# Attention and routed feed-forward on one core: slots in partitions, centred keys, token tiles of 128, ranks from sign counts

## The chip, the cores and the metric

The kernel runs on one core of one Trainium2 chip. A core has five engines that take their instructions in order and wait for each other through semaphores: PE (TensorE, matmul), DVE (VectorE), ACT (ScalarE), POOL (GpSimd) and SP, which here only issues transfers. The metric is device time in microseconds (us) of one execution.

## What is computed

Eight batches, eight heads, 576 tokens, head dimension 64, 32 memory slots. Keys and values are summed into slots, every token attends over the 32 slots, the heads are joined to rows of 512, and the 128 best rows of each batch go through a two-layer feed-forward network.

```python
a = np.exp(phi - np.max(phi, axis=2, keepdims=True))
a = a / (np.sum(a, axis=2, keepdims=True) + 1e-09)
k_m = np.einsum('bhsm,bhsd->bhmd', a, k)
v_m = np.einsum('bhsm,bhsd->bhmd', a, v)
scores = scale * np.matmul(q, k_m.transpose(0, 1, 3, 2))
scores = scores - np.max(scores, axis=-1, keepdims=True)
attn = np.exp(scores)
attn = attn / (np.sum(attn, axis=-1, keepdims=True) + 1e-09)
x = np.matmul(attn, v_m)              # then heads joined: (B, S, 512)
gate = np.einsum('bsd,d->bs', x, w_gate)
top_idx = np.argpartition(-gate[b], capacity)[:capacity]      # per batch, capacity 128
xe = x[b, top_idx]
ye = np.maximum(xe @ w1, 0.0) @ w2    # w1 512x1024, w2 1024x512
out[b, top_idx] = xe + sigmoid(gate[b, top_idx])[:, None] * ye
```

## The kernel before

The program has three stages. In the first, 16 groups (a batch and four heads) go through a long softmax of phi on DVE (`softmax`) and a sum of keys into slots (`keys`, L298), two groups at a time; `values(0)` sums the values of batches 0 to 3 beside the second half of them. In the second stage `values(1)` does the same for batches 4 to 7 while batches 0 to 3 go through attention and feed-forward. In the third, batches 4 to 7 go through attention and feed-forward with nothing beside them.

`values` is 144 steps of 16 matmuls (L336, four row strips of 32 rows each); its operands come in 18 chunks of 8 steps from `vparts` and `aparts` in DRAM, through the queues of SP and POOL (L317, L323), two chunks in buffers.

A batch is a generator that runs from `yield` to `yield` (37 of them): `centre` (the mean of v_m over slots is taken apart as a high and a low row), then three times `scores` and `attend` (two columns of 96 tokens each), `rank`, `gather`, `ffn1`, `ffn2`. In `scores` tokens lie in partitions: 16 matmul instructions (L405; every fp32 matmul in the code is two instructions on PE), a maximum, a subtraction, Exp and Tanh (exp(s)-1 is built as (exp(s)+1)·tanh(s/2)), a product, a sum and a reciprocal. In `attend` the result is transposed on PE (L445), copied by ACT (L447), multiplied with the centred values (L453), scaled by DVE (L456), the two mean rows are added by POOL (L460), and DVE takes the product with w_gate and its sum (L430, L432, L435). `rank` counts for each token the tokens above it (L487) and the equal ones before it (L489); `gather` turns ranks into indices (L500, L505) and fetches the 128 rows; `ffn1` takes their gate again, transposes them (L530) and multiplies with w1 (L539, hidden units in partitions), `ffn2` with w2 (L552).

The order on every engine is the order in which the generators are advanced: `turns(jobs, 10, 3)` gives each of up to three live batches one step per round and starts a new one at the earliest 10 rounds after the last; in the second stage `beside(..., sums, 1)` puts one step of `values` behind every step of a batch. All matmul results but those of `values` share four PSUM banks (`bank`). "Column" below is a group of tokens; "step" is what lies between two yields.

## Time and profile before

| | us |
|---|---|
| time, median of 3 runs (1300.88 to 1302.33) | 1301.61 |
| the profiled execution's own time | 1302.55 |
| its span in the trace | 1300.8 |
| first stage, up to the last key sum | 652 |
| second stage, up to the end of batch 3 | 652 to 1016.3 |
| third stage, batches 4 to 7 | 1016.3 to 1296.4 |

The span is the time from the program's first instruction to its last; the profiled execution's own time is 1.75 us longer. The stage ends are the ends of instructions in the trace: the last matmul of L298, and the feed-forward result (L556) of batch 3 and of batch 7. The granted clock of PE is given as a share of 2.4 GHz, so that 0.50 is its lower level, 1.2 GHz, and 1.00 its upper; the trace's first record of a change is at 840 us, and the column says 1.00 for all that lies ahead of that.

### The profile page before, as it was taken

The page shows a single profiled execution, that of the slowest core. Times are in us where ns is not written, and L with a number is a line of the kernel's source. Part 1 is how long each engine was busy: PE and PEld are TensorE (multiplying, and loading weights), DVE is VectorE, ACT ScalarE, POOL GpSimd, SP SyncE. Part 2 cuts the span into 40 slices and gives each one's busy share as a digit, 9 for nine tenths or more (in the row PEclk, how much of TensorE's full clock was granted, in tenths as well). Part 3 has the DMA queues.
Part 4 walks back from the last instruction along what each step waited for, and adds up shares of the span by engine and source line. Part 5 has one row for each costly group of instructions (what it writes and reads, how often), then busy time and mean ns, then how long its engine had stood idle before and what let it go on. Part 6 is the DMA issues. An engine that isn't in the chain of part 4 may idle for free. (4 is left out here: it accounts for less than half of the span.)

```text
span 1300.8 us, 16837 instructions
## 1 busy us (share of the span) xinstructions
PE 691.2 (53%) x6656; PEld 589.1 (45%) x6656; DVE 875.1 (67%) x1480; ACT 272.0 (21%) x489; POOL 406.5 (31%) x489
## 2 busy tenths in 40 slices
PE   0021022221248877773209989879986653557646
PEld 0011011111148767663108778758766443436524
DVE  8978799999789999999703465543524467664551
ACT  1222133333133333333102111101100221012100
POOL 7133332111244324421232343533440034321230
PEclk9999999999999999999999999975895766677677
DMA  5799871211379996962185565553660121100010
GB/s 191 287 319 365 305 265 46 58 34 54 94 157 193 185 195 145 199 143 53 37 247 133 139 135 130 122 132 87 145 179 21 33 61 41 40 21 21 29 33 17
DMA packets 119934, 165.48 MB, mean 127 GB/s; under 512 B 84912, under 2 KB 86960, under 8 KB 115248
## 3 DMA queue, kind: packets, MB, share of 16 engines
q1 hardware_dynamic: 93360, 84.69, 26.9%
q0 software_dynamic: 26496, 79.72, 20.5%
q8 instruction: 53, 0.87, 0.3%
q14 instruction: 25, 0.20, 0.1%
HBM read 105.64 MB, written 68.16 MB: 134 GB/s over the span
## 5 line engine op out<-in xcount | busy, mean ns | idle before, releaser
L336 PE MATMUL acc<-v_rows,a_rows 32*128 32x128 f32 x4608 | 255.4, 396 | 92.4 <-DMA a_rows<-aparts 92.4
L336 PEld LDWEIGHTS acc<-v_rows,a_rows 32*128 32x128 f32 x4608 | 237.6, 305 | 123.2 <-issue 109.3
L276 PE MATMUL bank<-ident,e 128*96 128x128 f32 x96 | 23.9, 422 | 345.8 <-DVE e L245 345.8
L276 PEld LDWEIGHTS bank<-ident,e 128*96 128x96 f32 x96 | 16.8, 193 | 348.7 <-issue 300.0
L460 POOL TENSOR_TENSOR xj<-xj,mean 96x1024 f32<-96x1024 f32 x48 | 118.1, 2465 | 126.5 <-DVE xj L456 108.9
L323 POOL DMA_DIRECT2D a_rows<-aparts x144 | 90.1, 633 | 214.2 <-PE acc L336 202.6
L288 POOL DMA_DIRECT2D aparts<-alo x64 | 47.7, 746 | 238.4 <-DVE alo L284 212.2
L298 PE MATMUL bank<-aS,kb 96*128 96x64 f32 x384 | 86.1, 423 | 11.6 <-ACT aS L278 11.6
L298 PEld LDWEIGHTS bank<-aS,kb 96*128 96x128 f32 x384 | 83.1, 331 | 16.4 <-ACT aS L278 15.7
L453 PE MATMUL bank<-vbd,eT 128*96 128x256 f32 x192 | 76.4, 551 | 14.0 <-ACT eT L447 14.0
L539 PE MATMUL bank<-xeT,w_sb 128*128 128x128 f32 x512 | 77.6, 325 | 8.5 <-ACT xeT L533 8.5
L539 PEld LDWEIGHTS bank<-xeT,w_sb 128*128 128x128 f32 x512 | 75.5, 239 | 12.0 <-ACT xeT L533 11.7
L430 DVE TENSOR_TENSOR prod<-xj,wg 96x1024 f32<-96x1024 f32 x24 | 37.8, 1574 | 47.0 <-POOL xj L460 47.0
L456 DVE TENSOR_TENSOR xj<-bank,rd 96x512 f32<-96x512 f32 x48 | 32.4, 682 | 53.4 <-PE bank L453 53.4
L405 PE MATMUL bank<-kbd,qb 128*96 128x64 f32 x384 | 58.6, 337 | 0.0
L410 DVE TENSOR_REDUCE smx<-bank 96x16 f32<-96x512 f32 x24 | 16.3, 678 | 61.3 <-PE bank L405 61.3
L405 PEld LDWEIGHTS bank<-kbd,qb 128*96 128x96 f32 x384 | 56.4, 249 | 1.9
L552 PE MATMUL bank<-w_sb,hT 128*128 128x512 f32 x128 | 56.6, 595 | 0.0
L556 DVE SCALAR_TENSOR_TENSOR ye<-bank,gr,xe 128x512 f32<-128x512 f32 x8 | 6.0, 750 | 74.2 <-PE bank L552 74.2
L453 PEld LDWEIGHTS bank<-vbd,eT 128*96 128x96 f32 x192 | 40.9, 232 | 31.3 <-ACT eT L447 15.1
L190 DVE SCALAR_TENSOR_TENSOR lo<-num,vh 128x576 f32<-128x576 f32 x48 | 36.2, 755 | 21.7 <-ACT vh L151 21.7
L505 PE MATMUL bank<-tok,pick 96*128 96x1 f32 x96 | 20.4, 340 | 56.9 <-DVE pick L500 56.9
(131 smaller groups left out, 1374.2 us busy)
## 6 DMA issues: line engine op xcount, KB each, us to landing
v_rows<-vparts SPq DMA_DIRECT2D x72, 512.0 KB, 6.1
vparts<-vb POOLq DMA_DIRECT2D x32, 576.0 KB, 5.5
vparts<-vhi POOLq DMA_DIRECT2D x32, 576.0 KB, 7.2
kb<-in_k SPq DMA_DIRECT2D x16, 576.0 KB, 7.7
vb<-in_v SPq DMA_DIRECT2D x16, 576.0 KB, 6.3
aparts<-aparts POOLq DMA_DIRECT2D x32, 288.0 KB, 3.2
a_rows<-aparts SPq DMA_DIRECT2D x144, 64.0 KB, 7.1
a_rows<-aparts POOLq DMA_DIRECT2D x144, 64.0 KB, 6.4
```

Source lines behind the costliest of these rows:

```text
L190: stt(out=lo, in0=val, scalar=GRID, in1=h, op0=ALU.mult, op1=ALU.subtract)
L276: nc.tensor.transpose(out=tp[:, c], in_=a[:, (c0 + c) * PT:(c0 + c + 1) * PT], identity=ident)
L288: nc.gpsimd.dma_start(out=aparts[r, u, b, part, 0].rearrange("(c p) m -> p c m", p=PT), in_=src[:, :, h * M:(h + 1) * M])
L298: nc.tensor.matmul(out=km[:, rr], lhsT=kb[:, c, rr * P:(rr + 1) * P], rhs=aS[:, c, rr * 2 * M:(rr + 1) * 2 * M], start=(c == 0), stop=(c = ...
L323: (nc.sync, nc.gpsimd)[u].dma_start(out=a_rows[ch % 2][2 * r + u::8, :, r].bitcast(F32), in_=aparts[r, u, b0:b0 + SET].rearrange("b t w s ...
L336: nc.tensor.matmul(out=accs[bb][:, :P].rearrange("p (u d) -> p u d", d=Dh), lhsT=ar[p, s].rearrange("p r m -> p (r m)"), rhs=vr[p, :, s], ...
L405: nc.tensor.matmul(out=sc[:, c, :, r], lhsT=qb[:, r, c * PT:(c + 1) * PT], rhs=kbd[b][:, r], start=True, stop=True)
L430: nc.vector.tensor_mul(prod[:n, :cols], rows, wg[:n].unsqueeze(1).to_broadcast([n, cols, D]))
L453: nc.tensor.matmul(out=o[:, u].rearrange("p r d -> p (r d)"), lhsT=eT[:, c, u], rhs=vbd[b % 3][:, u], start=True, stop=True)
L460: nc.gpsimd.tensor_add(x, x, t.unsqueeze(1).to_broadcast([PT, 2, D]))
L539: nc.tensor.matmul(out=ps[:, f, :n], lhsT=w1_sb[:, d, (f0 + f) * P:(f0 + f + 1) * P], rhs=xeT[:, d, :n], start=(d == 0), stop=(d == KD - 1))
L552: nc.tensor.matmul(out=ps[:n], lhsT=hT[:, f, :n], rhs=w2_sb[:, f], start=(f == 0), stop=(f == KF - 1))
```

## The change

The attention part is laid out anew, with slots in partitions.

- `centre` subtracts from k_m its mean over the slots (three DVE operations), so that scores come out centred, and no maximum is taken. The small remainder of the value mean is cut into three bf16 pieces by POOL (`los`), which PE adds to each output with one bf16 matmul (`ones3`, `rest`); the large part is one row, added by POOL.
- `scores` has k_m as the stationary operand and 288 tokens as the moving one: per batch 16 matmul instructions (L452), each with 64 output partitions, ACT reads them from PSUM (four Exp, four Tanh), and DVE's product lands as the transposed tile `eT`. The PE transposes of L445 and ACT's copies of L447 are gone.
- `attend` takes the sums over slots on PE (`den`, 20 instructions with 4 columns) and works on five tiles of 128 tokens, the last one half filled.
- `rank` counts with ACT's Sign, five times, and with DVE's comparison for equal, five times. `gather` brings the gate along with the index, so that the gate of the fetched rows isn't taken again.
- `ffn` multiplies with w1 with tokens in partitions (16 instructions of 512 columns instead of 64 of 128), transposes the result on PE and copies it by ACT. w1 and w2 are cut by a `yield` after every four instructions.
- Batches start 14 rounds apart instead of 10; a batch has 39 yields. The first step of `values(1)` now stands ahead of batch 0's first transpose on PE.
- At the end a count (`good`) says whether any sum over slots was too large; then all engines read it and, if it was, jump into a second path (`general=True`) that takes every batch again with a maximum.

The core of the diff (removed lines are the functions above):

```diff
-    for t in kbd + vbd:
+    vls = [const.tile([P, NPR, 2, M], F32, name=f"vls{i}") for i in range(2)]
+    for t in kbd + vbd + vls:
         nc.gpsimd.memset(t, 0.0)
...
     def late_consts():
...
+        nc.vector.tensor_copy(ident16, ident)
...
+        for t in tgs:
+            nc.gpsimd.memset(t, 0.0)
+            nc.gpsimd.iota(t[:, :, 0], pattern=[[P, NT]], base=0, channel_multiplier=1,
+                           allow_small_or_imprecise_dtypes=True)
...
     def centre(b):
+        heads = kbd[b].rearrange("p r (u m) -> p (r u) m", u=2)
+        km = work.tile([P, H], F32, name="kmean")
+        nc.vector.tensor_reduce(km, heads, axis=AX.X, op=ALU.add)
+        nc.vector.tensor_scalar_mul(km, km, 1.0 / M)
+        nc.vector.tensor_sub(heads, heads, km.unsqueeze(2).to_broadcast([P, H, M]))
+        yield
...
+        los = work.tile([P, NPR, 3], BF16, name="los")
+        for i in range(3):
+            nc.gpsimd.tensor_copy(los[:, :, i], lo)
+            if i < 2:
+                nc.gpsimd.tensor_sub(lo, lo, los[:, :, i])
+        yield
...
+    def expm1(dst, s, shape):
+        e = step.tile(shape, F32, name="es")
+        d = step.tile(shape, F32, name="th")
+        nc.scalar.activation(e, s, AF.Exp, scale=scale)
+        nc.scalar.activation(d, s, AF.Tanh, scale=scale / 2)
+        yield
+        nc.vector.scalar_tensor_tensor(out=dst, in0=e, scalar=1.0, in1=d,
+                                       op0=ALU.add, op1=ALU.mult)
+    def scores(b):
+        N = S // 2
+        for j in range(2):
+            qb = qs.pop((b, j))
+            for g in range(2):
+                sc = bank([P, N])
+                for rr in range(2):
+                    nc.tensor.matmul(out=sc[rr * 2 * M:(rr + 1) * 2 * M], lhsT=kbd[b][:, 2 * g + rr],
+                                     rhs=qb[:, 2 * g + rr], start=True, stop=True)
+                yield from expm1(eTs[b % 2][:, g, j * N:(j + 1) * N], sc, [P, N])
...
+    def attend(b, general):
...
+        den = bank([P, NT, 2, 4])
+        for c in range(NT):
+            for g in range(2):
+                nc.tensor.matmul(out=den[:, c, g], lhsT=eT[:, g, c * P:(c + 1) * P], rhs=heads_of,
+                                 start=True, stop=True)
+        yield
...
+        for c0 in range(0, NT, 2):
+            cols = min(2, NT - c0)
+            x = step.tile([P, 2, D], F32, name="xj", bufs=3)[:, :cols]
+            for c in range(cols):
+                o = bank([P, D])
+                nc.tensor.matmul(out=o, lhsT=ones3, rhs=rest, start=True, stop=False)
+                for g in range(2):
+                    nc.tensor.matmul(out=o[:, g * 4 * Dh:(g + 1) * 4 * Dh],
+                                     lhsT=eT[:, g, (c0 + c) * P:(c0 + c + 1) * P],
+                                     rhs=vbd[b % 3][:, g], start=False, stop=(g == 1))
+                yield
...
+            nc.gpsimd.tensor_add(x, x, row.unsqueeze(1).to_broadcast([P, cols, D]))
+            yield
+            score(tg[:, c0:c0 + cols, 1], x, cols)
...
     def rank(b):
...
+        for c in range(NT):
+            g = tg[:, c, 1:2]
+            off = (NT - 1 - c) * P
+            nc.scalar.activation(sign, row, AF.Sign, bias=g, scale=-1.0,
+                                 accum_out=less[:, c:c + 1])
             nc.vector.scalar_tensor_tensor(
+                out=cmp, in0=row, scalar=g, in1=wide[:, off:off + S],
                 op0=ALU.is_equal, op1=ALU.mult, accum_out=equal[:, c:c + 1])
+            if c % 2:
+                yield
...
+    def ffn(b, t):
...
+        for f0 in range(0, F, 512):
+            ps = bank([P, 512])
+            for d in range(KD):
+                nc.tensor.matmul(out=ps[:n], lhsT=xeT[:, d, :n], rhs=w1_sb[:, d, f0:f0 + 512],
+                                 start=(d == 0), stop=(d == KD - 1))
+                if d % 2:
+                    yield
+            nc.scalar.activation(h[:n, f0:f0 + 512], ps[:n], AF.Relu)
         hT = one.tile([P, KF, P], F32, name="hT")
         for f0 in range(0, KF, 4):
+            turned(hT, h, f0, f0 + 4)
             yield
         ps = bank([P, D])
         for f in range(KF):
             nc.tensor.matmul(out=ps[:n], lhsT=hT[:, f, :n], rhs=w2_sb[:, f],
                              start=(f == 0), stop=(f == KF - 1))
+            if f % 2:
+                yield
...
+    def attention_and_ffn(b, general=False):
+        if not general:
+            for j in range(2):
+                load_q(b, j)
         yield from centre(b)
         yield
+        yield from (scores_less_max if general else scores)(b)
...
-    finish(beside(turns([batch(b) for b in range(SET)], 10, 3), sums, 1))
+    finish(beside(turns([attention_and_ffn(b) for b in range(SET)], 14, 3), sums, 1))
     finish(sums)
-    finish(turns([batch(b) for b in range(SET, B)], 10, 3))
+    finish(turns([attention_and_ffn(b) for b in range(SET, B)], 14, 3))
+    ps = bank([1, B])
+    nc.tensor.matmul(out=ps, lhsT=ones, rhs=good, start=True, stop=True)
...
+    taken = nc.values_load(any_bad[0:1, 0:1])
+    with tc.If(taken > 0):
+        for b in range(B):
+            finish(attention_and_ffn(b, True))
```

On PE in the third stage, before, around the feed-forward of one batch (xe, w_sb and hT are the feed-forward's; gate is another batch's ranks, kbd and es a third batch's scores, pick its ranks' selection):

```order
L475 MATMUL bank<-ident,gate 96x96 x6
L405 MATMUL bank<-kbd_90,qb 96x2x32 x8
L530 MATMUL bank<-ident,xe 128x128 x4
L539 MATMUL bank<-xeT,w_sb 128x128 x32
L445 MATMUL bank<-ident,es 128x96 x4
L552 MATMUL bank<-w_sb,hT 128x512 x8
L453 MATMUL bank<-vbd_92,eT 96x256 x4
L350 MATMUL bank<-ident,v_m_8604 128x128
L445 MATMUL bank<-ident,es 128x96 x4
L505 MATMUL bank<-tok,pick 128x1 x6
```

The same place after the change, w2 of one batch (L622) beside the scores of another (L452), and the rank transposes of a third (L538) with their selection (L575) behind:

```order
L452 MATMUL bank<-qb,kbd_90 64x288 x2
L622 MATMUL bank<-w_sb,hT 128x512 x2
L538 MATMUL bank<-ident,tg_128 128x128 x4
L538 MATMUL bank<-ident,tg_128 128x64
L452 MATMUL bank<-qb,kbd_90 64x288 x2
L622 MATMUL bank<-w_sb,hT 128x512 x2
L452 MATMUL bank<-qb,kbd_90 64x288 x2
L622 MATMUL bank<-w_sb,hT 128x512 x2
L452 MATMUL bank<-qb,kbd_90 64x288 x2
L622 MATMUL bank<-w_sb,hT 128x512 x2
L575 MATMUL bank<-tg_128,pick 128x2 x5
```

Before, w1 and w2 of a batch stand as one piece each; now w2 is in four pieces with the scores of another batch between them, and the transposes of L445 are gone.

On DVE, the end of the last batch's ranks before (cmp above and cmp equal in turn):

```order
L489 SCALAR_TENSOR_TENSOR cmp,equal<-row,gate,wide 96x288
L487 TENSOR_SCALAR cmp,above<-row,gate 96x576
L489 SCALAR_TENSOR_TENSOR cmp,equal<-row,gate,wide 96x384
L487 TENSOR_SCALAR cmp,above<-row,gate 96x576
L489 SCALAR_TENSOR_TENSOR cmp,equal<-row,gate,wide 96x480
L487 TENSOR_SCALAR cmp,above<-row,gate 96x576
L489 SCALAR_TENSOR_TENSOR cmp,equal<-row,gate,wide 96x576
L493 TENSOR_TENSOR above<-above,equal 96x6
L500 TENSOR_TENSOR pick<-iota_r,above 96x768
```

and a batch's ranks on DVE after the change:

```order
L485 TENSOR_REDUCE tg_126<-four 128x1
L556 SCALAR_TENSOR_TENSOR cmp,equal<-row,tg_126,wide 128x576 x5
L562 SCALAR_TENSOR_TENSOR less<-less,equal 128x5
L570 TENSOR_TENSOR pick<-iota_r,less 128x640
L579 TENSOR_SCALAR idx<-bank 128x1
L587 TENSOR_SCALAR gr<-gr 128x1
L627 SCALAR_TENSOR_TENSOR ye<-bank,gr,xe 128x512
```

The counts of the tokens above have left DVE for ACT, and between the index and `ye` the gate of the fetched rows is no longer taken.

On PE at the program's end, after the change (before, it ends with L552 and a branch):

```order
L611 MATMUL bank<-w_sb,xeT 128x512 x8
L600 MATMUL bank<-ident,h 128x128 x8
L622 MATMUL bank<-w_sb,hT 128x512 x8
L708 MATMUL bank<-good,ones 1x8
L714 TENSOR_LOAD any_bad
L715 COMPARE_AND_BRANCH
```

A matmul, a load and a compare stand behind the last feed-forward; the load waits for the last transfers of all queues, and it and the compare stand at the end of every engine.

## Rows read from the trace of the kernel before

**Rows 1.** The page: busy time by engine, and PE's granted clock in 40 slices

```profile
PE 691.2 (53%) x6656; PEld 589.1 (45%) x6656; DVE 875.1 (67%) x1480; ACT 272.0 (21%) x489; POOL 406.5 (31%) x489
...
PEclk9999999999999999999999999975895766677677
```

**Rows 2.** Busy us by stretch: stretch, its length, engines, granted clock, DMA share, GB/s

```profile
0.00:652.00 652.00, 236.23 (x2783) 224.28 (x2783) 569.81 (x848) 188.98 (x307) 206.50 (x323) 1.00 0.60 166
652.00:690.00 38.00, 8.16 (x93) 6.56 (x92) 2.91 (x14) 2.97 (x9) 9.49 (x15) 1.00 0.90 252
690.00:840.00 150.00, 141.66 (x1381) 116.20 (x1378) 77.95 (x152) 20.80 (x43) 62.53 (x58) 1.00 0.57 131
840.00:1016.30 176.30, 148.85 (x1624) 118.15 (x1623) 70.38 (x149) 18.95 (x42) 51.96 (x49) 0.76 0.43 104
1016.30:1296.40 280.10, 156.27 (x784) 123.91 (x783) 154.03 (x317) 40.26 (x88) 75.02 (x44) 0.70 0.11 33
```

**Rows 3.** PE's waits from 1000 us on: total us, times, longest

```profile
PE bank L505 <- DVE pick L500: 45.7, 4, 15.6
PE bank L475 <- DVE gate L435: 35.6, 5, 9.8
PE bank L453 <- ACT eT L447: 14.0, 6, 4.8
```

**Rows 4.** Timeline of PE: start us, us, what, [idle before <-releaser]

```profile
682.61 1.97 PE L336 MATMUL acc<-v_rows,a_rows 32*128 32x128 f32 x32 [29.84 <-DMA a_rows<-aparts]
...
701.30 2.02 PE L453 MATMUL bank<-vbd,eT 128*96 128x256 f32 x4
703.25 1.12 PE L336 MATMUL acc<-v_rows,a_rows 32*128 32x128 f32 x16
704.30 0.47 PE L350 MATMUL bank<-ident,v_m 128*128 128x128 f32 x1
...
711.93 2.82 PE L405 MATMUL bank<-kbd,qb 128*96 128x64 f32 x16
...
720.72 0.90 PE L445 MATMUL bank<-ident,es 96*128 96x96 f32 x4
...
833.80 6.45 PE L539 MATMUL bank<-xeT,w_sb 128*128 128x128 f32 x29 [0.69 <-ACT xeT L533]
...
847.89 7.13 PE L552 MATMUL bank<-w_sb,hT 128*128 128x512 f32 x16
854.96 1.11 PE L336 MATMUL acc<-v_rows,a_rows 32*128 32x128 f32 x32
...
873.08 2.69 PE L505 MATMUL bank<-tok,pick 96*128 96x1 f32 x12 [4.69 <-DVE pick L500]
...
885.07 1.09 PE L389 MATMUL bank<-ident,vsum 128*96 128x128 f32 x4
```

**Rows 5.** Groups by line, shapes apart: busy us, mean ns | idle before

```profile
L460 POOL TENSOR_TENSOR xj<-xj,mean 96x1024 f32<-96x1024 f32 x48 | 118.1, 2465 | 126.5 <-DVE xj L456 108.9 <-issue 15.7
L487 DVE TENSOR_SCALAR_CACHE_REDUCE cmp<-row,gate 96x576 bf16<-96x576 f32 x48 | 37.7, 785 | 4.8 <-ACT row L477 4.3
L417 DVE SCALAR_TENSOR_TENSOR es<-es,d 96x512 f32<-96x512 f32 x24 | 16.4, 684 | 38.9 <-ACT d L415 38.9
L151 ACT ACTIVATE vh<-num,c 128x576 int16<-128x576 f32 x16 | 12.4, 774 | 10.1 <-DVE num L180 10.1
L164 DVE TENSOR_SCALAR ph<-ph,mx 128x576 f32<-128x576 f32 x16 | 22.3, 1397 | 0.6
```

**Rows 6.** Timeline: DVE's start, and the last batch's end

```profile
4.77 14.45 DVE L164 TENSOR_SCALAR ph<-ph,mx 128x576 f32<-128x576 f32 x1
...
1276.62 1.11 PE L530 MATMUL bank<-ident,xe 128*128 128x128 f32 x4 [4.63 <-DMA xe<-out,idx]
1295.62 0.75 DVE L556 SCALAR_TENSOR_TENSOR ye<-bank,gr,xe 128x512 f32<-128x512 f32 x1 [16.86 <-PE bank L552]
1296.65 1.02 POOL L558 DMA_INDIRECT out<-ye,idx  x1 [22.40 <-DVE ye L556]
```

More of the change, by code (lines that the diff above doesn't have):

```diff
@@ L57 @@
     PT = S // NC
-    NJ = qT.shape[1]
-    NPR = qT.shape[3]
+    NPR = qT.shape[2]
+    NT = -(-S // P)
+    tiles = [min(P, S - c * P) for c in range(NT)]
     NG = phiT.shape[1]
@@ new lines, in centre @@
+        yield
+        rest = work.tile([3, D], BF16, name="rest")
+        tp = bank([3, NPR, P], BF16)
+        for r in range(NPR):
+            nc.tensor.transpose(out=tp[:, r], in_=los[:, r], identity=ident16)
+        nc.scalar.activation(rest, tp.rearrange("p r d -> p (r d)"), AF.Copy)
+        mean[b] = row, rest
+    st = {}
+    def expm1(dst, s, shape):
[6 more added lines that the diff above has]
+                                       op0=ALU.add, op1=ALU.mult)
@@ new lines, in rank @@
+    def rank(b):
+        tg = tgs[b % 3]
+        row = one.tile([P, S], F32, name="row")
+        for c0 in range(0, NT, 4):
+            cc = range(c0, min(c0 + 4, NT))
+            ps = bank([P, 4 * P])
+            for c in cc:
+                n = tiles[c]
+                nc.tensor.transpose(out=ps[:, (c - c0) * P:(c - c0) * P + n],
+                                    in_=tg[:n, c, 1:2].to_broadcast([n, P]),
+                                    identity=ident[:n, :n])
+            n = sum(tiles[c] for c in cc)
+            nc.scalar.activation(row[:, c0 * P:c0 * P + n], ps[:, :n], AF.Copy)
+        yield
+        less = work.tile([P, NT], F32, name="less")
+        equal = work.tile([P, NT], F32, name="equal")
+        sign = one.tile([P, S], BF16, name="sign")
+        cmp = one.tile([P, S], BF16, name="cmp")
+        for c in range(NT):
[3 more added lines that the diff above has]
+                                 accum_out=less[:, c:c + 1])
+            nc.vector.scalar_tensor_tensor(
+                out=cmp, in0=row, scalar=g, in1=wide[:, off:off + S],
+                op0=ALU.is_equal, op1=ALU.mult, accum_out=equal[:, c:c + 1])
+            if c % 2:
+                yield
+        yield
+        nc.vector.scalar_tensor_tensor(out=less, in0=less, scalar=-0.5, in1=equal,
+                                       op0=ALU.mult, op1=ALU.add)
+        st[b, "rank"] = less
```

292 lines of the change are left out of this document (121 added, 171 removed).

## The prediction

> **What bounds the kernel now.** I read the page first, then busy time by stretch, then waits and the timeline of PE. The page [rows 1] shows no engine near its limit over the span (DVE 67%, PE 53%), so each stage is read by itself [rows 2]. The first is DVE's: 569.8 of 652 us. The change leaves it alone. In the second, PE first waits 29.8 us for its operands (682.61) [rows 4], and from 690 to 840 it is busy 141.7 of 150 us, from 840 to 1016.3 for 148.9 of 176.3, while DVE has about half the time: PE sets the pace. In the third none does: PE is busy 156.3 of 280.1 us, DVE 154.0, POOL 75.0 [rows 2]. There PE waits 45.7 us for rank selections, 35.6 us for gates and 14.0 us for the copied transposes [rows 3], behind chains of DVE, POOL and ACT. So in the second stage the change is worth what it does to PE, in the third also what it takes from the chains.
>
> PE has two prices, by its clock. The granted clock reads 1.00 up to 840 us only because nothing is recorded there: four L453 take 1.95 us at 701.30 (to the next row's start), and 32 of L336 take 1.11 us at 854.96 where 16 took 1.05 us at 703.25 [rows 4]. Up to about 840 PE ran at the lower level, 1.2 GHz, busy with L336 and short pieces of attention between them; the level rose during the first w1 matmuls, which began at 833.80 [rows 4]. Behind that the granted clock is 0.76 on average to 1016.3 and 0.70 in the third stage [rows 2], which is the upper level for 52% and 40% of the time.
>
> **PE's work.** In lower-level us per batch, from [rows 4], before: scores 48 x 0.172 (2.75/16) = 8.3; L445 12 x 0.21 = 2.5; L453 24 x 0.488 = 11.7; w1 64 x 0.222 = 14.2; w2 16 x 0.88 (twice 7.07/16, measured at the upper level) = 14.1; selection 12 x 0.224 = 2.7; 20 other transposes x 0.26 (L389) = 5.2. Sum 58.7. With 144 steps of 1.05 us, 151, the second stage comes to 386; the trace's busy time there, its upper-level share counted twice, is 141.7 + 148.9 x 1.52 = 368, so the prices are good to 5%.
>
> After: den 20 x 0.224 (L505's price, as few columns) = 4.5; outputs 5 x (1.95 + 0.44 for the bf16 matmul, half an L552) = 12.0; w1, now of w2's shape, 14.1; w2 14.1; selection 10 x 0.224 = 2.2; 28 transposes x 0.26 (5 of ranks, 8 of h new) = 7.3. Scores are 16 instructions of 288 columns: by L453's price per column 0.549 each, 8.8; but two neighbours write different halves of the array's outputs. No row shows that; the nearest is L336, four of which with a quarter of the rows each go in 0.26 us. I take the halves as overlapping, 4.4, since that row is nearest in kind. Sum 58.6, or 63.0 without overlap (35 lower-level us over eight batches, some 22 us of time).
> The Trainium skill, "TensorEngine Tiling (Array Packing)", Key Properties, says that such tiles work in parallel but that a change of tiling mode drains the engine; here every score step changes mode. By its first half the sum is the one taken; no row here prices the drain.
>
> So PE's work stays the same. What changes is its clock and its idle time.
>
> **The other engines.** DVE has 154.0/4 = 38.5 us per batch. It loses three of four passes over scores (each three times about 0.684, L417's shape; 6.2), most of L417 itself (0.5), L487 (6 x 0.86 with its accumulator read, 5.2) and the second gate (about 1.9), gains 2 in centre and den, and sweeps five tiles instead of six: about 26. POOL has 18.8 and loses 3.5 of 6 adds of 2.46 us [rows 5]: about 11 with `los`. ACT has 10 and gains five Signs of about 0.85 (0.774 for 576 columns [rows 5] and an accumulator read): about 14. All stay under PE's 29 (upper) to 59 (lower).
>
> **First stage and start of the second: +6 us.** DVE's first instruction is now the copy of `ident16`. The first L164 took 14.45 us, the other fifteen about 0.52 [rows 5, 6], while POOL filled its buffers. The copy will sit there in its place, with the maximum and L164 behind it: +2 (0 to 5). Then 0.8 MB more of q goes ahead of the first operands on SP: at 252 GB/s [rows 2] 3.2 us, with issue 4. PE starts at 688.6 instead of 682.6. The POOL memsets of `eT` wait for the end of the first stage as the copies ahead of them do: nothing.
>
> **Second stage: 17 us less.** The first w1 comes behind 45 steps of `values` instead of 72, since batches start 14 rounds apart: 45 x 1.05 = 47.3, batch 0's work without feed-forward 28.3, batch 1's first 16 steps 19.0, idle 4; with 5 us of w1 until the clock rises (6 at 833.80) that is 792. Of 386 lower-level us 286 are left, plus 28 idle as before in 840 to 1016.3 (176.3 - 148.9). With the clock shared as before, 52% upper, (286 + 28)/1.52 = 207: batch 3 ends at 999 instead of 1016. A step of `values` stands between every two pieces of w1 (3.5 us each), which can keep the level low; den is one more long row of small matmuls like the selection, during which PE was at the lower level at 873.08 [rows 4]. Against that, PE has fewer gaps. Bounds for the share: 0.25 (+45 us) and 0.75 (-27).
>
> **Third stage: 74 us less.** PE's busy time stays 156 x 58.6/58.7. Idle was 124. It should fall to 50: 12 while batch 4 is alone (centre is a chain of DVE operations that PE waits for), 10 in the next 14 rounds, 5 for each of two rounds with three batches (selection waits behind `ye`), 4 and 14 at the drain, where the last batch's fetch (4.6 us [rows 6]), copies and ReLU stand alone. Gates and ranks now have PE work of two other batches to hide them, and their chains are shorter by L487, half the POOL adds and the second gate. Bounds 30 to 124. 156 + 50 = 206.
>
> **The end: +5 us.** After the last `ye` every engine waits for the last scatter (4.4 us to the span's end now, as before), then loads a register, compares and jumps over the second path. No row shows these; the nearest are a semaphore step of under 0.1 us and a fetched gather of 4.6 us. I take one such round trip, 5, since all of it is serial; bounds 0 and 10.
>
> Sum: 999 + 206 + 4.4 + 5 = 1214 us of span; with 1.75 around it 1216 for a profiled execution, whose like now is 0.9 above the median: **1215**.
>
> **Rivals.**
> 1. *The clock stays low in the second stage.* The steps of `values` between the pieces of w1 keep PE at 1.2 GHz to the end of batch 3, as from 690 to 840, where PE hardly paused. Then 314 us follow 792: 1106, and 1322 in all: slower. It decides at an upper-level share below 7%. For it: w1 ran in pieces of 6 us before and in 3.5 now. Against it: at 833.80 the level rose within one such piece [rows 4], and pieces of 3.5 us with 1 us between are most of PE's time there. 6%.
> 2. *Hand-offs stay.* With four banks and in-order queues PE's idle time in the third stage stays 124: 999 + 280 + 10 = 1289. For it: `ye` still stands ahead of the next selection on DVE. Against it: the chains lose half their work. 9%.
> 3. *PE at the upper level throughout,* now that gaps are few: 386/2 + 32 from 688.6, 913, then 117 + 50, and the end: 1090. Against it: 690 to 840, where it was 94% busy at the lower level. 4%.
> The Trainium skill, "TensorE: Matmul & The Clock Gate", "Why this matters for your kernels", promises the upper level to an engine kept busy without gaps; the stretch from 690 to 840 [rows 2] speaks against it as a rule for small matmuls, and I leave it this rival's 4%.
> 4. *It doesn't do what it says:* the count finds a bad sum and the second path runs, eight batches one after the other, over 2000 us. The sums are 32 and a small rest here. 1%.
>
> **How the numbers follow.** The forecast has 80%. Its own range is 1165 (share 0.75 and 30 idle, about) to 1275 (share 0.25, no overlap of scores' halves in part). To 1290 it takes in rival 2; outside are rivals 1, 3 and 4 and some 7% of the forecast. A measurement tells 0.2% from no change (2.6 us). Faster 92%, slower 7% (rivals 1 and 4), within 1%.
>
> **What would show it.** PE's first operand wait should end near 689; the first w1 at about 787; batch 3's result at 999, batch 7's at 1205; PE idle 50 us in the third stage, with the waits for selection and gates gone from the top; four neighbouring score instructions in 1.1 us at the lower level (2.2 without overlap); DVE near 26 us per batch. Wrong would be: a granted clock of 0.5 through 800 to 1000, PE waiting for DVE as long as now, or a tail of over 15 us behind the last `ye`.

## The result, and the profile after

| | before | after |
|---|---|---|
| time, median of four runs, us | 1301.24 | 1172.95 |
| lowest and highest, us | 1299.97, 1302.33 | 1165.39, 1177.25 |
| ratio to before, 95% interval | | 0.901 (0.896 to 0.906) |
| profiled execution's span, us | 1300.8 | 1175.4 |
| PE's first step of `values(1)`, us | 682.6 | 687.4 |
| end of batch 3, of batch 7, us | 1017.1, 1296.4 | 974.6, 1165.9 |

The change saves 128 us, 9.9%; 87 were forecast. The time lies near the lower end of the forecast's range. The ends of batches here are the ends of the feed-forward's last DVE instruction, 0.75 us behind its start (the 1016.3 us given ahead for batch 3 is its start). The profiled execution, to which all traces of the change belong, is the slowest of its four. The page after, in the lines that answer to [rows 1]:

```profile
PE 662.3 (56%) x6138; PEld 492.3 (42%) x6138; DVE 765.7 (65%) x1283; ACT 293.0 (25%) x561; POOL 351.3 (30%) x529
...
PEclk9999999999999999999999999999577987598897
```

Busy time by stretch, as [rows 2]: first stage, PE's wait for its operands, second stage up to the first recorded rise of the clock, its rest up to batch 3's end, third stage, tail. Columns: stretch, length, busy us of PE, PEld, DVE, ACT and POOL, granted clock, DMA share, GB/s.

```profile
0.00:654.20 654.20, 236.39 (x2784) 224.40 (x2784) 568.80 (x849) 189.09 (x307) 209.44 (x337) 1.00 0.59 165
654.20:687.40 33.20, 0.37 (x2) 0.19 (x2) 1.04 (x3) 0.44 (x2) 9.72 (x17) 1.00 0.90 254
687.40:783.00 95.60, 93.56 (x888) 69.58 (x888) 37.27 (x83) 15.61 (x40) 26.79 (x40) 1.00 0.59 139
783.00:974.65 191.65, 182.80 (x1949) 116.13 (x1945) 60.73 (x131) 37.20 (x89) 57.97 (x79) 0.83 0.57 132
974.65:1165.90 191.25, 149.15 (x525) 81.98 (x525) 97.62 (x217) 50.62 (x123) 46.39 (x56) 0.81 0.16 52
1165.90:1175.40 9.50, 0.00 (x0) 0.00 (x0) 0.23 (x3) 0.00 (x0) 0.99 (x1) 0.65 0.11 37
```

PE's idle time is what is to be seen: 8.8 of 191.7 us in the second stage behind 783 us (before 27.5 of 176.3 from 840 us on), 42.1 of 191.3 in the third (before 123.8 of 280.1), at a higher granted clock (0.83 and 0.81 for 0.76 and 0.70). PE's waits from 1000 us on, as [rows 3]:

```profile
PE bank L575 <- DVE pick L570: 10.9, 4, 5.3
PE bank L411 <- DVE vls L401: 8.5, 3, 6.5
PE bank L600 <- DMA xe<-out,idx: 5.4, 1, 5.4
PE bank L538 <- DVE tg L485: 5.0, 2, 3.4
```

The selection (L575, before L505) went from 45.7 to 10.9 us, the gates (L538, before L475) from 35.6 to 5.0, and the copied transposes (14.0) are gone. The third stage after begins 25 us ahead of this window; with them the only wait that grows is L411's, for the centring of values, to 13.6 us, and it is then the largest. PE's timeline at the start of the second stage, as [rows 4]:

```profile
687.42 1.12 PE L353 MATMUL acc<-v_rows,a_rows 32*128 32x128 f32 x16 [32.85 <-DMA a_rows<-aparts]
...
698.16 1.23 PE L452 MATMUL bank<-qb,kbd 128*64 128x288 f32 x4
699.32 1.12 PE L353 MATMUL acc<-v_rows,a_rows 32*128 32x128 f32 x16
...
707.85 4.43 PE L493 MATMUL bank<-heads_of,eT 128*128 128x4 f32 x20
712.20 1.12 PE L353 MATMUL acc<-v_rows,a_rows 32*128 32x128 f32 x16
713.12 0.65 PE L510 MATMUL bank<-rest,ones 3*128 3x512 bf16 x1
713.70 2.08 PE L512 MATMUL bank<-vbd,eT 128*128 128x256 f32 x4
715.70 1.12 PE L353 MATMUL acc<-v_rows,a_rows 32*128 32x128 f32 x16
```

From start to start four score instructions (L452) take 1.16 us, the 20 of `den` 4.35, and an output tile (L510 and L512) 2.58.

**One sum for each stage.** In what follows "work" is PE's busy time with the part at the upper clock level counted twice, so in lower-level us, and "upper" is the busy time at the upper level; both come from the trace's clock records and the busy time between them. Then length = work - upper + idle. The work of two traces with the same instructions differs by up to 4% (401.9 us in the second stage of e7 below, which has the change's instructions there, and 386.3 in e2's). The forecast's upper is what its other numbers leave: 386 less the busy 278 (310.4 less 32 idle), and 234 less 156.

| | second stage: length | work | upper | idle | third stage: length | work | upper | idle |
|---|---|---|---|---|---|---|---|---|
| before | 334.5 | 382.7 | 84.7 | 36.5 | 279.3 | 226.9 | 70.7 | 123.1 |
| forecast | 310.4 | 386 | 108 | 32 | 206 | 234 | 78 | 50 |
| after | 287.2 | 399.5 | 123.1 | 10.9 | 191.3 | 244.4 | 95.3 | 42.1 |
| e3 chains back | 290.9 | 398.8 | 118.5 | 10.6 | 221.5 | 244.7 | 87.0 | 63.8 |
| e4 before, order of after | 333.3 | 392.6 | 100.5 | 41.1 | 258.9 | 226.9 | 75.5 | 107.6 |
| e6 scores by tokens | 372.1 | 416.2 | 83.8 | 39.7 | 235.5 | 266.4 | 93.1 | 62.1 |
| e9 the same with a yield | 337.5 | 422.6 | 116.3 | 31.2 | 239.0 | 265.2 | 86.2 | 60.0 |
| e10 pauses | 318.7 | 407.6 | 120.8 | 31.9 | 222.1 | 248.4 | 87.6 | 61.3 |

### The profile page after: what moved, and what is told of

It reads as the page before. It is cut to its first block, busy times and chain, and to the rows that moved or that the text cites. A ratio compares the mean times of both kernels' runs of the same rounds, so it can differ in the third digit from the quotient of the medians.

```text
span 1175.4 us, 15823 instructions
## 1 busy us (share of the span) xinstructions
PE 662.3 (56%) x6138; PEld 492.3 (42%) x6138; DVE 765.7 (65%) x1283; ACT 293.0 (25%) x561; POOL 351.3 (30%) x529
## 5 line engine op out<-in xcount | busy, mean ns | idle before, releaser
L611 PE MATMUL bank<-w_sb,xeT 128*128 128x512 f32 x128 | 73.0, 709 | 3.4 <-ACT xeT L602 3.4
L519 POOL TENSOR_TENSOR xj<-xj,mean 128x1024 f32<-128x1024 f32 (+1 forms) x24 | 47.7, 1988 | 73.0 <-DVE xj L516 72.9
L512 PE MATMUL bank<-vbd,eT 128*128 128x256 f32 x160 | 66.4, 556 | 0.0
L516 DVE TENSOR_TENSOR xj<-bank,rd 128x512 f32<-128x512 f32 x40 | 27.6, 689 | 56.8 <-PE bank L512 56.6
L622 PE MATMUL bank<-w_sb,hT 128*128 128x512 f32 x128 | 62.3, 620 | 0.2 <-ACT hT L602 0.2
L480 DVE TENSOR_TENSOR prod<-xj,wg 128x1024 f32<-128x1024 f32 (+1 forms) x24 | 25.1, 1046 | 46.6 <-POOL xj L519 46.6
L211 DVE TENSOR_TENSOR low<-low,lo 128x576 f32<-128x576 f32 x64 | 48.5, 758 | 2.2
L305 POOL DMA_DIRECT2D aparts<-ahi x64 | 47.7, 745 | 2.1 <-DMA a_rows<-aparts 1.6
L209 DVE TENSOR_TENSOR lo<-lo,rh 128x576 f32<-128x576 f32 x64 | 48.0, 750 | 0.0
L512 PEld LDWEIGHTS bank<-vbd,eT 128*128 128x128 f32 x160 | 38.4, 265 | 18.7 <-issue 13.7
L556 DVE SCALAR_TENSOR_TENSOR cmp<-row,tg,wide 128x576 bf16<-128x576 f32 x40 | 32.7, 817 | 17.7 <-ACT row L542 16.8
```

Of the source, the lines that this page charges most:

```text
L209: tt(out=lo, in0=lo, in1=rh, op=ALU.mult)
L211: tt(out=low, in0=low, in1=lo, op=ALU.add)
L305: nc.gpsimd.dma_start(out=aparts[r, u, b, part, 0].rearrange("(c p) m -> p c m", p=PT), in_=src[:, :, h * M:(h + 1) * M])
L512: nc.tensor.matmul(out=o[:, g * 4 * Dh:(g + 1) * 4 * Dh], lhsT=eT[:, g, (c0 + c) * P:(c0 + c + 1) * P], rhs=vbd[b % 3][:, g], start=False, ...
L516: nc.vector.tensor_mul(x[:, c].rearrange("p (h d) -> p h d", d=Dh), o.rearrange("p (h d) -> p h d", d=Dh), rd[:, c0 + c].unsqueeze(2).to_b ...
L519: nc.gpsimd.tensor_add(x, x, row.unsqueeze(1).to_broadcast([P, cols, D]))
```

## The experiments

Each starts from the changed kernel unless its heading says otherwise; times are medians of four runs or five, ratios are to the kernel before, run beside them.

### Order or chains

The prediction gave PE's lost idle time two reasons at once, another batch's work beside each wait and shorter chains on DVE, POOL and ACT. Four kernels take them apart.

**e1.**

```diff
-    finish(turns([attention_and_ffn(b) for b in range(SET, B)], 14, 3))
+    finish(turns([attention_and_ffn(b) for b in range(SET, B)], 10, 3))
```

(the same for the second stage)

> The changed kernel (1173 us) with batches started 10 rounds apart again instead of 14. Theory A (order: PE lost its idle time because the longer lag and the cut pieces put another batch's work beside every wait): the lag is half of that, so PE's idle time in the third stage goes from 42 back to 70 to 90 us and the time to 1205 to 1230. Theory B (chains: it lost it because DVE, POOL and ACT have less to do per batch): idle stays within 10 us of 42 and the time at 1165 to 1185.

1172.9 us, 0.902 (0.899 to 0.905): no difference. Idle in the third stage is 41.0 us. Theory B's side: the longer lag gives nothing here.

**e2.**

```diff
-                if d % 2:
-                    yield
             nc.scalar.activation(h[:n, f0:f0 + 512], ps[:n], AF.Relu)
+            yield
...
-            if f % 2:
-                yield
+        yield
```

> The changed kernel with w1 in two pieces and w2 in one again (no yields inside them, as in the kernel before). Theory A (order): while a piece of 7 us runs, two other batches wait for PE and afterwards PE waits for them, PE's idle time in the third stage is 60 or more and the time 1195 to 1215. Theory B (chains): 1165 to 1185. For the clock: if it is pieces cut by steps of values that hold it down, the share at the upper level in the second stage rises from 0.66 to 0.75 or more and the time falls by some 10 us.

1181.5 us, 0.909 (0.906 to 0.912): 9 us longer, inside B's numbers. Idle in the third stage rises by 8 us to 50.6, so the cut pieces are worth that much. The second stage got shorter (279.0 us), with upper at 123.4 as in the change: pieces cut by steps of `values` do not hold the clock down.

**e3.**

```diff
-            nc.scalar.activation(sign, row, AF.Sign, bias=g, scale=-1.0,
-                                 accum_out=less[:, c:c + 1])
+            nc.vector.tensor_scalar(out=sign, in0=row, scalar1=g, scalar2=0.0,
+                                    op0=ALU.is_gt, op1=ALU.add, accum_out=less[:, c:c + 1])
...
+        score(gr, xe.unsqueeze(1), 1)
+        nc.scalar.activation(gr, gr, AF.Tanh, scale=0.5)
...
+            nc.gpsimd.tensor_add(x, x, nil.unsqueeze(2).to_broadcast([P, cols, D]))
             nc.gpsimd.tensor_add(x, x, row.unsqueeze(1).to_broadcast([P, cols, D]))
```

> The changed kernel with the chains of before put back beside PE: the tokens above are counted by DVE instead of ACT, the gate of the fetched rows is taken again on DVE, and POOL adds twice per pair of tiles (a zero the first time). PE's instructions and their order stay. Theory A (order): PE's idle time in the third stage stays within 15 us of 42, time 1170 to 1190. Theory B (chains): most of the idle time comes back, 42 to 90 or more, and the time is 1220 or more.

1208.0 us, 0.925 (0.920 to 0.931): 35 us longer, between the two theories' numbers. The second stage hardly notices (290.9 us, idle 10.6). In the third, idle rises from 42.1 to 63.8. PE's waits there:

```profile
PE bank L411 <- DVE vls L401: 20.3, 4, 9.5
PE bank L539 <- DVE tg L485: 19.2, 6, 4.5
PE bank L576 <- DVE pick L571: 13.8, 4, 6.9
```

The gates' wait comes back (19.2 us for 5.0), the selection's hardly (13.8 for 10.9). Against 45.7 and 35.6 us [rows 3] that is a small part.

**e4**, from the kernel before:

```diff
-    finish(turns([batch(b) for b in range(SET, B)], 10, 3))
+    finish(turns([batch(b) for b in range(SET, B)], 14, 3))
...
+                if f == 1:
+                    yield
...
-        yield
+            if f % 2:
+                yield
         ye = one.tile([P, D], F32, name="ye")
```

> The kernel before (1301 us) with the order of the change alone: batches 14 rounds apart, a yield inside each half of w1 and three inside w2. Theory A (order): PE's idle time in the third stage falls from 123 to 60 or less and the time to 1220 to 1250. Theory B (chains): idle stays above 100 and the time at 1280 or more.

1273.2 us, 0.978 (0.974 to 0.981). Idle in the third stage stays above 100 us (107.6), as B says, though the time is 7 us below its bound. The order alone is worth 28 us to the kernel before. Neither reason carries 128 us, and the second stage is at its old length (333.3 us) in e4 and at its new one in e1, e2 and e3.

### The clock, and where the rest is

**e5.** w1 as before, with hidden units in partitions and without the transposes of h:

```diff
...
-            ps = bank([P, 512])
-            for d in range(KD):
-                nc.tensor.matmul(out=ps[:n], lhsT=xeT[:, d, :n], rhs=w1_sb[:, d, f0:f0 + 512],
+            ps = bank([P, 4, P])
+            for f in range(4):
+                for d in range(KD):
+                    nc.tensor.matmul(out=ps[:, f, :n],
+                                     lhsT=w1_sb[:, d, (f0 + f) * P:(f0 + f + 1) * P],
+                                     rhs=xeT[:, d, :n], start=(d == 0), stop=(d == KD - 1))
...
```

> The changed kernel with w1 as before: hidden units in partitions, 64 instructions of 128 columns per batch instead of 16 of 512, no transposes of h, the same yields. PE has 8 transposes per batch less (17 lower-level us in all). Theory C (shape: the upper level of the clock, 127 of 287 us in the second stage and 63% of the third against 92 and 39% before, comes from w1's long rows): the upper level falls to about 95 us of the second stage and 45% of the third, time 1200 to 1220. Theory D (pauses: it comes from PE pausing less, whatever the shape): shares stay and the time is 1155 to 1170.

1175.8 us, 0.905 (0.902 to 0.908): no difference. The upper level holds for 124.7 us of the second stage (126.8 in the change) and 54% of the third, between the two theories there. The time gives theory C no support: w1's shape is not where the gain is.

**e6.** `yield from scores_less_max(b)` for every batch, `load_q` by tiles of 128 tokens, and

```diff
...
-            qb = step.tile([P, NPR, S // 2], F32, name="qb", bufs=3)
-            nc.sync.dma_start(out=qb[:, :, :n], in_=qT[b, :, :, c * P:c * P + n])
+            if c + 2 < NT:
+                load_q(b, c + 2)
+            qb = qs.pop((b, c))
...
```

> The changed kernel with the scores of the second path for every batch: tokens in partitions, five tiles instead of four half-columns, a maximum and a subtraction on DVE and two transposes on PE per tile, so that one more hand-off PE to DVE to PE stands in each step (q loaded two tiles ahead). Theory E (the slots-in-partitions layout is where the rest of the gain is, after lag and chains were put back with 0 and 35 us): PE idle in the third stage 42 to 75 or more, time 1225 or more. Rival (the hand-offs have another batch's work beside them in any case): only PE's and DVE's added work shows, 10 more transposes at 0.26 lower-level us per batch (some 15 us of time in all), time 1180 to 1195.

1295.5 us, 0.995 (0.993 to 0.997): with this one part undone nearly all of the gain is gone, 122.5 us, 85 of them in the second stage. PE's waits from 690 to 1030 us:

```profile
PE bank L474 <- DVE es L471: 21.1, 20, 1.1
PE bank L577 <- DVE pick L572: 8.6, 3, 6.0
PE bank L540 <- DVE tg L487: 2.6, 1, 2.6
```

In each score step PE waits about 1 us for the subtraction, and waits for selection and gates, of which the change shows only 1.5 us there, are back with the rank chains unchanged. By the sum the second stage loses 17 us to work, 29 to idle and 39 to the clock. Part of the clock is lost inside the feed-forward; PE's timeline at the first batch's w1 (L613):

```profile
831.23 1.98 PE L613 MATMUL bank<-w_sb,xeT 128*128 128x512 f32 x4
...
837.79 0.41 PE L474 MATMUL bank<-ident,es 128*128 128x128 f32 x2 [1.07 <-DVE es L471]
838.13 0.67 PE L354 MATMUL acc<-v_rows,a_rows 32*128 32x128 f32 x16
838.73 3.45 PE L613 MATMUL bank<-w_sb,xeT 128*128 128x512 f32 x4
```

Four instructions take 1.98 us ahead of the wait of 1.07 us and 3.45 from 0.9 us behind it on. e6 is not the kernel before, whose three score steps of two columns have yields between their parts; it says what this version of the layout costs, its added instructions on PE and DVE included.

**e9.** e6, and

```diff
             nc.vector.tensor_sub(dd, sc[:n], mx[:n].unsqueeze(2).to_broadcast([n, H, M]))
+            yield
             tp = bank([P, 2, P])
```

> e6 (scores by tokens, 1295.5 us) with a yield between the subtraction on DVE and the two transposes on PE that wait for it, so that work of values and of other batches stands in between; PE's instructions are the same in number and shape. Theory D (PE's pauses keep the clock low: in e6 it waits 20 times for about 1 us in each stage): idle falls from 40 and 62 us to some 15 and 45, the upper level rises from 93 to some 125 us of the second stage, and the time is about 1205 to 1225. Theory F (it is the small matmuls of the scores themselves that keep the clock low, 64 columns and 128-column transposes in place of 288 columns): idle falls as much, the upper level stays at some 93 us of the second stage, and the time is 1245 to 1265.

1272.8 us, 0.979 (0.974 to 0.983): outside both theories' numbers. The level comes back in the second stage, 126.7 us, as D says; idle falls only to 31.2 us, and the third stage gains nothing (239.0 us). PE's waits from 690 to 1050 us:

```profile
PE bank L578 <- DVE pick L573: 9.1, 3, 6.0
PE bank L541 <- DVE tg L488: 8.9, 2, 5.8
PE bank L412 <- DVE vls L402: 7.7, 2, 5.1
```

The pause for the subtraction has gone to the selection, the gates and the centring of values. Theory F falls for the second stage, since shapes and numbers are those of e6; in the third the level does not come back (86 us for 93).

**e10.**

```diff
-                yield from expm1(eTs[b % 2][:, g, j * N:(j + 1) * N], sc, [P, N])
+                half = eTs[b % 2][:, g, j * N:(j + 1) * N]
+                wait = expm1(half, sc, [P, N])
+                for _ in wait:
+                    pass
+                nc.tensor.transpose(out=bank([P, P]), in_=half[:, :P], identity=ident)
+                yield
```

> The changed kernel (scores by slots, 1173 us) with four pauses of PE per batch: in each of the four score steps one transpose of a part of the finished product, read by nobody, stands on PE right behind the step's matmuls and waits for ACT and DVE, some 2 us; the yield comes behind it. Shapes of the scores stay, PE's work grows by 4 transposes per batch (8 lower-level us in all). Theory D: besides some 35 us more idle in each stage the upper level falls from 127 to 95 us or less of the second stage and the time rises to 1260 or more. Theory F: the upper level stays within 10% and the time rises by the idle alone, to 1210 to 1245.

1249.4 us, 0.961 (0.958 to 0.964), 76 us longer; its profiled execution is the fastest of the four, 1237.8 us. PE's wait from 690 to 1010 us:

```profile
PE bank L458 <- DVE eT L441: 22.0, 16, 1.5
```

Against the change's trace the two stages are 62 us longer: 40 us of idle, 12 of work and 10 less of upper. The upper level holds for 133.4 us of the second stage and 123.1 of the third (126.8 and 119.6 in the change). So in these traces the pauses' cost is mostly their own length, and theory D, that they keep the clock low, falls in these numbers; F's bound of 1245 us is 4 too low. The medians lie 76 us apart and the traces 62, because the change's trace is its slowest execution and e10's the fastest; the other 14 us are not accounted for.

What pauses do inside the feed-forward is seen in busy time and granted clock (the last column but two) from the first batch's first w1 to the end of its w2. In each of the four nothing is recorded ahead of the first rise, 4 to 5 us into the window, so that it reads 1.00 there. In the change:

```profile
778.60:822.20 43.60, 42.64 (x527) 25.40 (x523) 17.04 (x40) 12.06 (x29) 15.12 (x25) 1.00 0.73 167
```

In e6:

```profile
824.10:880.30 56.20, 51.95 (x536) 32.84 (x532) 19.44 (x39) 9.79 (x32) 14.64 (x21) 0.82 0.49 108
```

In e9:

```profile
831.10:873.60 42.50, 42.05 (x530) 26.68 (x526) 15.73 (x31) 9.23 (x28) 14.59 (x21) 1.00 0.61 137
```

In e10:

```profile
791.40:843.90 52.50, 47.10 (x531) 27.39 (x528) 17.02 (x41) 12.06 (x29) 15.95 (x26) 0.93 0.64 149
```

In the change and e9, with 1.0 and 0.5 us idle, the level stays up from its rise to the stretch's end; in e6, with 4.3 us idle, it is 0.82, and in e10, with 5.4 us, 0.93. So pauses there can cost the level, but their sum doesn't tell how much. What sets it stays open.

Part of the difference comes with no change of the program at all. Up to the end of batch 3, e3, e7 and e12 issue the change's matmuls on PE in the same order but for the score steps of e12, and yet their first recorded rise lies at 799.6, 736.9 and 779.7 us, the change's at 783.0. PE's score step in e7, and the same four instructions of the change at about that time:

```profile
739.80 0.71 PE L452 MATMUL bank<-qb,kbd 128*64 128x288 f32 x4
```

```profile
742.66 1.23 PE L452 MATMUL bank<-qb,kbd 128*64 128x288 f32 x4
```

Their "upper" in the second stage is 118.5 us (e3), 123.1 (the change), 129.4 (e12) and 132.5 (e7). So single traces of the same work differ by 14 us there: e9's 116.3 and e10's 120.8 can't be told from the change's by one trace, and only e6's 83.8 lies clear of them.

### Single costs

**e7.** The lines from the matmul over `good` to the end of the kernel are removed.

> The changed kernel without the check at the end: no matmul over the counts, no load of a register, no compare and no second path (the count itself stays). If the tail is the jump over the second path (PE's branch takes 4.36 us in the trace, the other engines go on 2.4 to 3.0 us after theirs), the time from the last feed-forward result to the span's end falls from 9.5 back to 4.4 us and the time by 5, to 1168. If the last scatter ends it anyway, less than 2 us.

1165.7 us, 0.895 (0.890 to 0.899). The tail behind the last `ye` is 5.0 us in its trace and 9.5 in the change's, so that 4.5 of the 7 us lie there. The rows of the jump in the change's trace (by the sequencers of the engines; ns least, median, most; first and last start):

```profile
L715 PEldq COMPARE_BRANCH x1: 4358/4358/4358, 1167.0 to 1167.0; - x1
...
L715 DVEq COMPARE_BRANCH x1: 72/72/72, 1167.5 to 1167.5; - x1
...
L715 DVEq EVENT_SEMAPHORE  x1: 21/21/21, 1170.5 to 1170.5; - x1
```

PE's branch takes 4.36 us; DVE's takes 0.07, but its next event comes 2.9 us behind it. The register load takes about 0.5 us, and it does not wait for the last scatter, as was said ahead of the prediction: it starts at 1166.4 us on PE, 0.4 behind the end of `ye`, while POOL is still issuing that scatter (L629).

```profile
L714 PEldq TENSOR_LOAD <-any_bad x1: 486/486/486, 1166.4 to 1166.4; - x1
```

```profile
1166.20 0.99 POOL L629 DMA_INDIRECT out<-ye,idx  x1 [22.54 <-DVE any_bad L713]
```

The Trainium skill, "Runtime: NRT & Kernel Launch", "Instruction fetch mechanics", says that a taken branch to a place that isn't fetched yet stalls until its page has come; these rows agree, and they give the price, but they do not show that the fetch is what PE waits for.

**e12.**

```diff
...
-                for rr in range(2):
-                    nc.tensor.matmul(out=sc[rr * 2 * M:(rr + 1) * 2 * M], lhsT=kbd[b][:, 2 * g + rr],
+            for rr in range(2):
+                for g in range(2):
+                    nc.tensor.matmul(out=scs[g][rr * 2 * M:(rr + 1) * 2 * M], lhsT=kbd[b][:, 2 * g + rr],
...
```

> The changed kernel with the eight score matmuls of a half of the tokens in another order: the two for the first half of the array's output columns (two instructions each), then the two for the second half, into two banks, where now first and second half alternate. In the trace four neighbouring score instructions take 1.16 us at the lower level. Theory G (neighbours on different halves run at the same time): only one of three borders lies between halves now, so that eight take about 3.0 us in place of 2.3, PE's work grows by 1.4 lower-level us per batch and the time by 5 to 10 us. Rival (an instruction with 64 output columns is cheap by itself, 0.29 us): eight take 2.3 us in this order too, and the time stays within 3 us.

1167.5 us, 0.898 (0.895 to 0.902). The timeline of PE, eight score instructions and what follows:

```profile
696.90 2.19 PE L452 MATMUL bank<-qb,kbd 128*64 128x288 f32 x8
699.03 1.97 PE L353 MATMUL acc<-v_rows,a_rows 32*128 32x128 f32 x32
```

Eight take 2.13 us where twice four took 2.32, so theory G's 3.0 doesn't come; the time is 5 us below the change's, not clear of noise. But the rival's reason, that such an instruction is cheap by itself, does not hold. PE's instructions that lie in the first half microsecond of a score step, in the change (698.16 to 698.69 us) and in e12 (696.90 to 697.43), and for comparison of an output tile (713.69 to 714.28 in the change):

```profile
698.16 0.75 PE L452 MATMUL bank<-qb,kbd 128*64 128x288 f32 x2
```

```profile
696.90 0.76 PE L452 MATMUL bank<-qb,kbd 128*64 128x288 f32 x2
```

```profile
713.70 0.80 PE L512 MATMUL bank<-vbd,eT 128*128 128x256 f32 x1
```

In both orders two score instructions start within 0.02 us of each other and run at the same time (together they last 0.75 us, and one alone 0.74); an instruction with 128 output columns starts alone. A pair costs 0.53 to 0.58 us (2.13/4, 1.16/2), about what L453's price gives for one instruction of 288 columns (0.55). So the overlap is there in e12's order too, and e12 can't separate the two explanations by its time: it had taken for granted that only direct neighbours overlap. The Trainium skill, "TensorEngine Tiling (Array Packing)", Key Properties, says that tiles work in parallel and that a change of mode drains: the pairs agree with the first half, though the records don't name the half that an instruction writes; no run here prices the drain.

### A faster version

**e8.**

```diff
-    finish(beside(turns([attention_and_ffn(b) for b in range(SET)], 14, 3), sums, 1))
-    finish(sums)
-    finish(turns([attention_and_ffn(b) for b in range(SET, B)], 14, 3))
+    def behind(b):
+        finish(sums)
+        yield from attention_and_ffn(b)
+
+    finish(beside(turns([attention_and_ffn(b) if b < SET else behind(b) for b in range(B)], 14, 3),
+                  sums, 1))
```

> The changed kernel with all eight batches in one row of turns: batch 4 starts as soon as one of three places is free and first finishes the sums of values, instead of waiting for the end of batch 3. In the change PE is alone with batch 3's feed-forward for 25 us (6 idle) and then with batch 4's start for 57 us (20 idle, upper level 23% of it). If these fills and drains are what is left to gain, 20 to 30 us go: 1143 to 1153. If the steps of values that batch 4 then waits for only move there, less than 10 us.

1157.7 us, 0.892 (0.888 to 0.896): 15 us less than the change, between the two expectations. Idle from the first step of `values(1)` to the last `ye` falls from 53 to 39 us.

**e11.** e8 with the edits of e1 and e5.

> e8 (all eight batches in one row of turns, 1157.7 us) with the lag of 10 and w1 in 128 columns, which are each worth between 3 us less and 3 us more by e1 and e5 (w1 without the 64 transposes of h is 17 lower-level us less of PE's work). If PE's work is what is left of the second stage, 1145 to 1155; if the lag alone sets when batch 4 can start, which waits for the end of batch 1 in any case, no difference from e8.

1150.1 us, 0.882 (0.877 to 0.887), the fastest of all: 8 us less than e8. Which of the two edits gives it wasn't taken apart.

## Why the prediction was right, and where it was off

- **Start, +6:** 4.8. The 2 us of the first stage came out by luck. DVE's last rows there start at 650.40 us and 648.39 before, but the copy of `ident16` is not why: it took 6.95 us, the operations behind it moved up, and DVE was 3.9 us ahead at its first long step. By its second group it was 1.8 us behind: of the 5.7 us that it lost, 4.96 are one wait for a transfer of v. Before, and after:

```profile
21.28 2.41 DVE L170 SCALAR_TENSOR_TENSOR ph<-q,ph 128x576 f32<-128x576 int16 x2
```

```profile
17.43 1.54 DVE L187 SCALAR_TENSOR_TENSOR ph<-q,ph 128x576 f32<-128x576 int16 x2
...
38.84 0.76 DVE L273 TENSOR_SCALAR vhi<-vb 128x1152 int32<-128x1152 int32 x1 [4.96 <-DMA vb<-in_v]
```

POOL's setup is longer by the new tiles, and its first transfer out of `vb` starts at 25.01 us instead of 22.24; that this kept a buffer of v from coming free is likely, not shown. From the last key sum PE waits 32.9 us, 2.8 longer (4 were said).
- **PE's work the same:** off by 4 lower-level us per batch. In the third stage it is 61.1 per batch (58.6 said), before 56.7 (58.7 said). The price of a score step was right (1.16 us for 1.1), and so was its reason, as far as the rows under e12 show it: two instructions run at the same time. No row ahead of the change could tell that from the bound of 2.2 us. An output tile costs 2.58 us for 2.39.
- **First w1 at 787, clock up at 792:** 778.6, and a level recorded from 783.0 us. That the level rises in the first w1 is not a rule of this kernel: e7 had it up from 736.9 to 747.2 us, with no w1 yet, and e3 only 22 us behind the first w1.
- **Second stage:** this step failed in size. Batch 3's end was to come 17 us earlier and came 42 earlier; by the sum above the stage was to be 24 us shorter and is 47. Idle is 21 us less than taken, upper 15 more, work 13 more. "28 idle as before" was the wrong term. Most of it was PE's waits on selection and gates, which I left because PE sets the pace. Before (840 to 1016 us), and after (783 to 975):

```profile
PE bank L505 <- DVE pick L500: 10.6, 3, 4.7
PE bank L475 <- DVE gate L435: 8.1, 2, 7.1
```

```profile
PE bank L575 <- DVE pick L570: 1.5, 3, 0.8
```

They went away, and by e3 and e1 neither shorter rank chains nor the lag did it. They come back in e6 and e9, with the scores by tokens. The layout takes the hand-off PE to DVE to PE out of each score step, and what DVE still has to do for a score is one product of 0.46 us. That DVE's queue, freed of steps that wait for PE, lets selection and gates through is the likely link; it is argued from these waits, not measured by itself.
- **Other engines:** DVE has 24.4 us per batch in the third stage (26 said), POOL 11.6 (11), ACT 12.7 (14).
- **Clock shared as before, 52%:** 66% behind the first rise, and 63% of the third stage where 39% was before. In the third stage upper was 95 us for 78 taken, which gave 17 us, idle gave 8 and work took 10 back: together the 15 us by which the stage is shorter than forecast.
- **Third stage, idle 124 to 50:** 42, near enough. Its split was wrong: gates, ranks and order were to give most of it. Undone alone, the rank and gate chains cost 22 us of idle (e3), the lag none, the cut pieces 8. Scores by tokens cost 20 of idle and 22 of work. The parts do not add up, and I can't share the 81 us out among them.
- **End, +5:** 9.5 us for 9.4, the right number from a wrong path. A round trip behind the last scatter was taken; the load (0.5 us) starts while the scatter is issued, and what makes the tail longer is PE's jump of 4.36 us.
- **Rivals:** none came. "Hand-offs stay" falls by the waits. "Upper level throughout" falls by the stretch to 783 us, busy 93.6 of 95.6 us: four score instructions at 698.16 take 1.23 us there, and the same four 0.71 us at 1050.51, where the granted clock is up. "The clock stays low" falls by the granted clock of 0.83.

So the forecast of a gain was right because PE's waits were rightly seen as the third stage's bound and PE as the second's. Over both stages the sums before and after say where the gain lies: idle falls by 107 us, upper rises by 63, and work rises by 34, so that they are 135 us shorter. The forecast was 42 us too small. The two stages give 38 of it: against the forecast idle is 29 us less (21 and 8), upper 32 more (15 and 17), and work takes 24 back. Idle and clock of the second stage had been taken as before, while the layout was priced by PE's instructions and by DVE's busy time.

Putting the scores back by tokens costs 100 to 122 us (e9, e6), which is nearly the whole gain. How much of that is PE's waiting for DVE inside a score step is not shown by itself, since e6 and e9 add work too: of the 129 us by which e6's two stages are longer, idle is 49, the clock 42 and work 39; of e9's 98, 38, 16 and 44. Four waits per batch put back alone cost 76 (e10). What stays open is the clock: e6 and e9 have the same matmuls and 93 and 127 us at the upper level in the second stage, while e10's pauses left it at 133.

## What to carry to other kernels

When a change takes a round trip between engines out of a step that every batch repeats, price the waits it ends at all places where the in-order queues hold others up, not only its instructions; "idle as before" is a forecast too. Undo the parts of a large change one at a time: here lag and w1's shape cost nothing when undone, the chains a quarter of the gain, and the layout of the scores nearly all of it; the parts need not add up to the whole. Where two stages have a fill and a drain each, try one row of turns before tuning their order (15 us here).

## What was not expected of the hardware

A jump over a long piece of code at the program's end costs about 4.5 us, most of it PE's 4.36 us. Two score instructions, with 64 output columns each, run at the same time, a pair in 0.53 to 0.58 us (under e12). The same matmuls can find PE's clock up in one execution and low in another (0.71 and 1.23 us for four score instructions). And a small DVE operation can wait out a POOL operation: `kmean` (L370), 8 numbers per partition, has a median of 2.18 us and takes 0.17 at the least. DVE's timeline in the change:

```profile
838.87 2.20 DVE L370 TENSOR_SCALAR kmean<-kmean 128x8 f32<-128x8 f32 x1
841.10 0.43 DVE L371 TENSOR_TENSOR kbd<-kbd,kmean 128x256 f32<-128x256 f32 x1
```

POOL's at the same time:

```profile
838.69 2.35 POOL L519 TENSOR_TENSOR xj<-xj,mean 128x1024 f32<-128x1024 f32 x1 [0.47 <-DVE xj L516]
```

L370 ends at 841.07 us, with the add of L519 at 841.04. Six of its eight runs take 2.2 us, and each of them ends 0.03 us behind such an add; in the other two, 0.20 and 0.17 us, POOL computes nothing. The next operation, with two inputs, takes its usual 0.43 us.
